# RWKV-7 attention with a gated feed-forward block: chunk 0's diagonal blocks re-laid by PE products, second inverse products on four tile places, a new written order

## The chip, the cores and the metric

The kernel runs on one core of one Trainium2 chip. The metric is the device time of one execution in microseconds (us), lower is better. Inputs and outputs are in DRAM; the core's engines are PE (TensorE, matrix products), DVE (VectorE), ACT (ScalarE), POOL (GpSimd) and SP (SyncE, which here only issues DMAs). Each engine works through its own instructions in the order in which they were written. A product on PE consists of loading a stationary operand (PEld) and streaming a moving one; results go to PSUM, from where DVE or ACT copy them to SBUF.

## The reference

```python
def _attn_ref(r, k, v, w, a, b):            # (4, 8, 768, 40) each
    state = np.zeros((B, H, D, D))
    for t in range(S):
        y[:, :, t] = np.einsum('bhd,bhde->bhe', rt, state)
        Sa = np.einsum('bhde,bhe->bhd', state, at)
        state_decay = state * wt[:, :, None, :] - np.einsum('bhd,bhe->bhde', Sa, bt)
        state = state_decay + np.einsum('bhd,bhe->bhde', vt, kt)
    return y

def _moe_ref(x, w_in, w_out):               # (3072, 320), (320, 2048), (2048, 320)
    h = x @ w_in
    g = h * (1.0 / (1.0 + np.exp(-h)))
    return g @ w_out
```

The attention output is re-ordered to (batch x time, head x channel) and goes through the feed-forward block. 32 pairs of batch and head each carry a state of 40 x 40 through 768 steps. w_in and w_out reach the kernel as 64-bit floats, which it turns into 32-bit ones on the chip.

## The kernel before, in words

**Chunks.** Time is cut into 12 chunks of 64 steps, and each chunk's recurrence is solved in closed form. `load` and `prepare` of a chunk bring its inputs, scan the decay (`down`, `between_`, `up`), scale a, b and k by it, and multiply them with each other (`between`): b with a gives, per pair of batch and head, a strictly triangular 64 x 64 matrix, kept in the tile sb. The chunk needs the inverse of one plus that matrix (tile X). `chain` then solves with X and updates the state G, `read` makes the chunk's output, `bring` re-lays it over DRAM as xt, and `moe` runs the feed-forward block on the 256 rows of the chunk: `full` and `rest` multiply with w_in (lines 1241 and 1254), `gate` applies the activation, `second` multiplies with w_out (line 1281). For chunk 0 the output goes to xt piece by piece from SBUF, without DRAM.

**The inverse.** It is made in one of two ways. Chunks 0 to 2 use `special`: the 16 x 16 blocks on the diagonal are re-laid so that each of 128 partitions holds one whole block. This re-laying is a trip through DRAM: eight DMAs write the blocks from sb to ms (line 543; for chunk 0 four of them go out on ACT's queue, all others on SP's), and one reads them as xs (line 711). DVE inverts the blocks with products and reductions (`dots`, lines 639 and 640) into the tile few, which is ZQ. The way back is a second trip: one DMA writes few to zs (line 719), eight read it into mi, a block-diagonal tile that POOL cleared at the start (line 725). From mi and the rest of sb three rounds of products with additions (`both`, `turn`, `more`; lines 749, 762, 794, 809) make X. For chunk 0 these rounds are cut in two halves. Chunks 3 to 11 are done in pairs by `inverse`: 32 x 32 blocks through DRAM (md, then mi), `dots` on DVE, and back through DRAM (zd, xd) into ZQ and X. `merge` then fills in the block below the diagonal with two groups of 32 products of 32 x 32 (two instructions each): `first` (line 875) and `second` (line 904), each followed by one copy on ACT and one on DVE (lines 257 and 261).

**Tile places.** A product of 32 x 32 uses one of 16 places of the PE array, given by its rows (where its inputs lie) and its columns (where its result goes). The products of `first` are on four places. The products of `second` take rows 32 or 96 and columns 0 or 64, two places in all.

**Weights.** `weights` fetches ten pieces of w_in and w_out as 64-bit words by POOL's DMA queue and turns them into 32-bit floats with steps on DVE and ACT (lines 334 to 370). For the first three pieces the final sum is made by PE with the identity matrix (line 358).

**What sets the order.** Every step is registered with `add` (engine, a cost for the planner, what it reads and writes). The steps get numbers in the order of these calls. The text ORDER lists all numbers in the order in which the instructions are written, and SLOTS gives each use of PSUM or of a rotating buffer its place. Both were searched beforehand by a planner and stand in the kernel as text; the kernel only follows them. So an engine's queue is ORDER restricted to that engine.

**The end.** A count of range checks is multiplied by ones on PE (line 1360) and DVE makes a flag of it (line 1355), which all engines read to skip a fallback path.

Of the kernel before, what the change touches and what calls it, by code (L numbers as in the profile page):

```python
# [10 lines left out]
F32 = mybir.dt.float32  # L11
# [120 lines left out]
"""  # L132

SLOTS = """
21031321312301233211210001321322331332101012301233132222321031202030032332001101131100100023213111111003001230
21301202301012100203001102130131313111033222231221000003311222122330211211120201021320313002303121311000011330
331223200231101300010200110112232231311130303203023110333221023113020311321110200021003021302
"""


@with_exitstack
def kernel(
    ctx: ExitStack,
    tc: tile.TileContext,
    aT: bass.AP,
    kT: bass.AP,
    bT: bass.AP,
    wT: bass.AP,
# [9 lines left out]
    nc = tc.nc  # L158
# [49 lines left out]
    mi = sb.tile([128, 32, 32], F32, name="mi")  # L208
    both_ = sb.tile([128, 2, 32, 32], F32, name="XI")
    XI, tmp = both_[:, 0], both_[:, 1]  # L210
    xs = sb.tile([128, 256], F32, name="xs")
    wc = ring("wc", 3, Q)
    ot = ring("ot", 1, DM)
    pairs = [ps.tile([128, 2, 512], F32, name=f"pair{i}") for i in range(4)]
# [1295 lines left out]
```

## Time and profile before

| | |
|---|---|
| runs of the kernel | 704.92, 702.89, 704.71 us |
| median | 704.71 us |
| the profiled execution | 703.18 us, of which its span is 701.4 us |
| mean granted PE clock in it | 0.997 |
| instructions in it | 27224 |
| moved by DMA | 77.14 MB in 117920 packets |

The profile page has the busy time of each engine, the span in 40 slices, the DMA queues, the chain of work that ended last, and the costliest groups of instructions by line. A row of a group reads: line, engine, operation, output and input tile, shapes, count, then busy time in us and mean duration in ns, then the idle time of the engine just before these instructions and what ended it. A row of the timeline gives the start and the length in us, then the same names; in brackets stands the idle time ahead. Matmul durations include the way through the array, so the distance from one start to the next is the measure of PE's pace. [...]

### The profile page before, as it was taken

To read this page: it belongs to the slowest core of one execution; us is meant where nothing else is said; L and a number is where in the kernel's file an instruction comes from. 1 tells how busy PE (TensorE), PEld (TensorE's weight loads), DVE (VectorE), ACT (ScalarE), POOL (GpSimd) and SP (SyncE) were. 2 spreads that over 40 slices of the span, in tenths; PEclk is the share of its full clock that TensorE was granted. 3 is DMA by queue.
4 is the path that set the end of the run, shared out by engine and by line. 5 is a ranking of instruction groups with operands and counts; after the bars stand their busy time and mean duration, and the time that the engine had idled before them with its cause. 6 is when DMAs were issued, how large, how long until landed. Compare 5 with 4: busy or idle time off the path is not lost.

```text
span 701.4 us, 27224 instructions
## 1 busy us (share of the span) xinstructions
PE 651.2 (93%) x12666; PEld 528.3 (75%) x12666; DVE 415.4 (59%) x612; ACT 194.8 (28%) x243; POOL 13.5 (2%) x31
## 2 busy tenths in 40 slices
PE   0449899999999999999998999999999999999996
PEld 0336688788778778878877778878788778787774
DVE  2887999993896366972447961538953971211000
ACT  4337146244013313114212214203313114021020
POOL 4000010000000000000000000000000000000000
PEclk9999999999999999999999999999999999999998
DMA  9665274763245364163542441642443222211101
GB/s 305 211 161 113 67 219 153 224 145 89 79 141 108 92 150 141 52 165 81 155 101 82 137 107 20 175 127 79 117 124 76 70 72 69 63 42 35 27 1 23
DMA packets 117920, 77.14 MB, mean 110 GB/s; under 512 B 65538, under 2 KB 114229, under 8 KB 117160
## 3 DMA queue, kind: packets, MB, share of 16 engines
q1 hardware_dynamic: 112900, 64.10, 34.7%
q0 software_dynamic: 2224, 10.63, 4.4%
q8 instruction: 101, 1.65, 1.0%
q10 hardware_dynamic: 2676, 0.59, 0.5%
q14 instruction: 19, 0.16, 0.1%
HBM read 60.29 MB, written 14.61 MB: 107 GB/s over the span
## 4 chain that ended last, share of the span: by engine, by line
PE 72%; DVE 10%; DMA 9%; SPq 4%; issue 2%; ACT 2%; ACTq 0%; POOL 0%; DVEq 0%; POOLq 0%
PE pair L1281 23%; PE pair L1241 22%; PE pair L1254 6%; PE pair L1159 3%; PE pair L1105 3%; PE pair L526 2%; DVE XI L639 2%; PE pair L1059 2%; DVE XI L640 2%; PE pair L1144 1%; DMA wz<-in_wT 1%; DMA gts<-in_w_in 1%; PE pair L1002 1%; PE pair L613 1%; PE pair L588 1%
## 5 line engine op out<-in xcount | busy, mean ns | idle before, releaser
L1281 PE MATMUL pair<-wo,gts 128*128 128x320 f32 x768 | 215.3, 436 | 0.2 <-issue 0.2
L1281 PEld LDWEIGHTS pair<-wo,gts 128*128 128x128 f32 x768 | 143.8, 190 | 57.6 <-issue 0.3
L1241 PE MATMUL pair<-xt,wi 128*128 128x256 f32 x768 | 175.4, 383 | 1.8 <-DVE ot L261 1.8
L1241 PEld LDWEIGHTS pair<-xt,wi 128*128 128x128 f32 x768 | 143.7, 190 | 23.8 <-DVE ot L261 1.9
L1264 ACT ACTIVATE gts<-pair 128x1024 f32<-128x1024 f32 x48 | 47.6, 1025 | 69.4 <-PE pair L1254 62.2
L640 DVE TENSOR_REDUCE XI<-XI 128x64 f32<-128x512 f32 (+9 forms) x85 | 58.6, 690 | 2.9
L1117 DVE TENSOR_TENSOR lam<-pair,ml 128x1024 f32<-128x1024 f32 x22 | 26.4, 1220 | 39.9 <-PE pair L1105 39.9
L1254 PE MATMUL pair<-xt,wi 64*128 64x256 f32 x384 | 48.5, 389 | 0.0
L261 DVE COPY ot<-pair 128x320 f32<-128x320 f32 x22 | 10.8, 489 | 62.8 <-PE pair L1281 55.8
L639 DVE TENSOR_TENSOR XI<-XI,mi 128x1024 f32<-128x1024 f32 (+8 forms) x60 | 33.5, 559 | 18.4 <-DMA mi<-md 16.6
L1254 PEld LDWEIGHTS pair<-xt,wi 64*128 64x128 f32 x384 | 35.4, 187 | 5.5 <-issue 0.7
L613 PEld LDWEIGHTS pair<-ident,kb 40*128 40x128 f32 x384 | 16.0, 148 | 20.6 <-DVE kb L508 11.1
L626 ACT COPY kt<-pair 128x640 f32<-128x640 f32 x24 | 16.6, 690 | 51.7 <-PE pair L613 48.9
L613 PE MATMUL pair<-ident,kb 40*128 40x40 f32 x384 | 17.2, 237 | 14.2 <-DVE kb L508 14.2
L508 DVE TENSOR_TENSOR kb<-kbv 128x512 f32<-128x512 f32 (+1 forms) x36 | 29.9, 861 | 0.3
L526 PE MATMUL pair<-a,kb 40*64 40x64 f32 x1536 | 28.4, 228 | 1.5 <-ACT kt L626 0.8
L526 PEld LDWEIGHTS pair<-a,kb 40*64 40x64 f32 x1536 | 25.8, 142 | 4.7 <-issue 1.9
L471 DVE TENSOR_TENSOR_SCAN kbv<-wz,zt 128x1024 f32<-128x1024 f32 x12 | 27.5, 2292 | 0.7
L1105 PEld LDWEIGHTS pair<-r,vut 40*64 40x64 f32 x1536 | 24.2, 135 | 4.5 <-issue 2.5
L489 DVE TENSOR_TENSOR_SCAN wz<-wz,zt 128x1024 f32<-128x1024 f32 x12 | 27.4, 2287 | 0.2
L358 PE MATMUL pair<-gts,ident 128*128 128x512 f32 x16 | 10.6, 767 | 18.0 <-ACT gts L338 18.0
L1105 PE MATMUL pair<-r,vut 40*64 40x64 f32 x1536 | 26.6, 220 | 0.4 <-issue 0.3
(149 smaller groups left out, 672.4 us busy)
## 6 DMA issues: line engine op xcount, KB each, us to landing
wz<-in_wT SPq DMA_DIRECT2D x12, 512.0 KB
kbv<-in_bT SPq DMA_DIRECT2D x12, 512.0 KB
kbv<-in_kT SPq DMA_DIRECT2D x12, 512.0 KB
a<-in_aT SPq DMA_DIRECT2D x12, 512.0 KB
r<-in_rT SPq DMA_DIRECT2D x48, 96.0 KB
vut<-in_vT SPq DMA_DIRECT2D x48, 96.0 KB
vu<-in_v SPq DMA_DIRECT2D x24, 160.0 KB
xh<-lam SPq DMA_DIRECT2D x22, 160.0 KB
```

Source lines behind the costliest of these rows:

```text
L471: nc.vector.tensor_tensor_scan(back(V), back(W[:, 2 : 2 + Q * C]), zt, 1.0, ALU.mult, ALU.add)
L489: nc.vector.tensor_tensor_scan(Z, Z, zt, 0.0, ALU.mult, ALU.add)
L508: TTn[engine].tensor_tensor(out=at_(kb, place(is_b, first), (576 * step, 4 // step), (128, 4), (1, C)), in0=blocks((kf, bf)[is_b]), in1=bl ...
L526: nc.tensor.matmul(room.tile[half(b), j, g * C : g * C + C], lhsT=kb[rows(j), place(is_b, q) : place(is_b, q) + C], rhs=A[rows(j), q * C : ...
L613: nc.tensor.matmul(pt.tile[:, j, g * D : g * D + D], lhsT=kb[rows(j), place(b, q) : place(b, q) + 2 * C], rhs=ident[rows(j), rows(j)], sta ...
L639: nc.vector.tensor_tensor(out=at_(tmp, 0, *dims), in0=x, in1=y, op=ALU.mult)
L640: nc.vector.tensor_reduce(out=out_, in_=at_(tmp, 0, *dims), axis=AX.X, op=ALU.add)
L1105: nc.tensor.matmul(pl.tile[half(1 - b if role else b), b, c * C : c * C + C], lhsT=vut[rows(b), role, hu, :], rhs=rs[rows(b), hh, :], star ...
L1241: nc.tensor.matmul(rooms[g].tile[:, f // 2, (f % 2) * T : (f % 2) * T + T], lhsT=wi[:, k, (4 * g + f) * 128 : (4 * g + f) * 128 + 128], rh ...
L1254: nc.tensor.matmul(rooms[g].tile[:, h, (f % 2) * T : (f % 2) * T + T], lhsT=wi3[half(h), g * 256 + (f % 2) * 128 : g * 256 + (f % 2) * 128 ...
L1264: nc.scalar.activation(out=gts[:, 4 * g * T : 4 * g * T + 4 * T], in_=rooms[g].tile.rearrange("p a b -> p (a b)"), func=AF.Silu)
L1281: nc.tensor.matmul(po[b].tile[:, 0, 0:DM], lhsT=g4[:, f, 128 * b : 128 * b + 128], rhs=wo[:, f, :], start=f == 0, stop=f == NF - 1,)
```

## The change

Four things are changed.

1. **Chunk 0's two trips through DRAM go.** The set TRIP holds the chunks that are treated the new way; it is (0,). `spread` multiplies columns of sb with columns of the identity matrix, in 64 products (128 instructions) on four places, so that each block lands on its partition in PSUM, in two interleaved sets of columns; ACT copies one set, scaled by a mask column of dm, to xs, and DVE adds the other, scaled by a second mask column. The way back: ACT copies the 256 results of few a second time next to themselves (`twice`), `gather` multiplies them with the identity, again 64 products, and one DVE product of 1024 elements with a mask writes mi in full. `masks` fills dm once on DVE. POOL's clearing of mi goes.
2. **The second inverse products** (`second` in `merge`) put their results at columns 64x + 32b instead of 64x, with the order of the loops changed so that neighbours use different places. The copies behind them become two copies of 256 elements each (`united`), on ACT and on DVE.
3. **ORDER and SLOTS are new** throughout. At the start of the new ORDER DVE's steps are: `masks`, then chunk 0's `down`, the scaling of b, `between_`, `up`, the scaling of a, and then the first weight step. In the old one the first weight piece's three steps of bit work and two of another piece stand ahead of chunk 0's `down`. The flag's product stands last on PE in the old ORDER, and before the last `rest` of chunk 9 in the new one.
4. **A variant that is not used** (ADDS is empty): additions in `more` by PE. `more` also names X among what it reads, which it did already in its first round.

```diff
-113 0 138 1 125 3 2 81 77 114 115 116 117 139 118 126 140 158 150 119 141 120 6 127 7 8 9 142 82 11 84 12 28
...
+102 24 0 147 1 114 2 3 70 72 6 9 7 71 8 10 103 14 104 105 15 106 25 148 107 11 115 26 127 108 139 27 73 20 41
...
-        nc.gpsimd.memset(mi, 0.0)
+        if 0 not in TRIP:
+            nc.gpsimd.memset(mi, 0.0)
...
+    TRIP, ADDS = (0,), ()
...
-        if n < NS:
+        if n in TRIP:
+            pass
+        elif n < NS:
...
+        if n in TRIP:
+            pt_ = Room("pair", 3)
+
+            def spread():
+                for t in range(16):
+                    for b in range(2):
+                        for c in range(2):
+                            nc.tensor.matmul(
+                                pt_.tile[64 * b + 32 * c : 64 * b + 32 * c + 32, 0, 32 * t : 32 * t + 32],
+                                lhsT=at_(sbs[i2][half(b)], 16 * c + t, (32, 32)),
+                                rhs=at_(ident[half(b)], 64 * b + 16 * c, (32, 2), (1, 16)),
...
+                                tile_position=(64 * b, 64 * b + 32 * c),
+                            )
...
+            def masks():
+                nc.vector.memset(dm, 1.0)
+                nc.vector.tensor_copy(out=dm[:, 0:3], in_=ml[:, 16:C:16])
+                nc.vector.tensor_tensor(out=dm[:, 1:4], in0=dm[:, 1:4], in1=ml[:, 16:C:16], op=ALU.subtract)
+                for r in range(2):
+                    nc.vector.tensor_reduce(out=dm[:, 4 + r : 5 + r], in_=ident[:, r:128:2], axis=AX.X, op=ALU.add)
...
+                lambda: nc.scalar.activation(out=at_(xs, 0, (16, 16), (1, 16)), in_=own(0), func=AF.Copy, scale=dm[:, 4:5]),
...
+                lambda: nc.vector.scalar_tensor_tensor(
+                    out=at_(xs, 0, (16, 16), (1, 16)), in0=own(1), scalar=dm[:, 5:6], in1=at_(xs, 0, (16, 16), (1, 16)), op0=ALU.mult, op1=ALU.add
+                ),
...
+        if n in TRIP:
+            pz = Room("pair", 2)
+
+            def twice():
+                nc.scalar.copy(out=few[:, 256:512], in_=few[:, 0:256])
+
+            def gather():
+                for t in range(16):
+                    for b in range(2):
+                        for r in range(2):
+                            nc.tensor.matmul(
+                                pz.tile[64 * b + 32 * r : 64 * b + 32 * r + 32, t // 8, t % 8 * C : t % 8 * C + C],
+                                lhsT=at_(few[half(b)], t, (16, 32)),
+                                rhs=ident[half(b), half(b)],
...
+                                tile_position=(64 * b, 64 * b + 32 * r),
+                            )
...
+                lambda: nc.vector.tensor_tensor(
+                    out=at_(DT, 0, (C, Q), (32, 2), (16, 2), (1, 16)),
+                    in0=at_(by_two(pz.tile), 0, (2, Q), (1, 2), (32, 2), (C, 16)),
+                    in1=at_(dm, 0, (0, Q), (2, 2), (1, 2), (0, 16)),
+                    op=ALU.mult,
+                ),
...
         def second():
-            for o in problems("b", "j", "m", "z", "x"):
+            for o in problems("j", "m", "z", "b", "x"):
...
-                    p2.tile[64 * x : 64 * x + 32, x, g * 32 : g * 32 + 32],
+                    p2.tile[64 * x + 32 * b : 64 * x + 32 * b + 32, x, g * 32 : g * 32 + 32],
...
-                    tile_position=(64 * x + 32, 64 * x),
+                    tile_position=(64 * x + 32, 64 * x + 32 * b),
...
+            def united(x=x, R_=R_):
+                for b in range(2):
+                    copy(
+                        ("ACT", "DVE")[x],
+                        X[R_, 8 * b : 8 * b + 8, 32:64],
+                        p2.tile[64 * x + 32 * b : 64 * x + 32 * b + 32, x, 256 * b : 256 * b + 256].rearrange("p (q t) -> p q t", q=8),
+                    )
```

More of the change, by code (lines that the diff above doesn't have):

```diff
@@ L74 @@
 ORDER = """
[57 rows of a table removed]
[56 rows of a table added]
 """
 SLOTS = """
-21031321312301233211210001321322331332101012301233132222321031202030032332001101131100100023213111111003001230
-21301202301012100203001102130131313111033222231221000003311222122330211211120201021320313002303121311000011330
-331223200231101300010200110112232231311130303203023110333221023113020311321110200021003021302
+03032311103303021222110101323023002212120312023311123033303013013000101212230032033133021000301100212123310230
+30212023120223123321310030031003013022110212013210201130302003211310312210110113020131012121113023100120202123
+13231301213030101300002211320113111230333021000112323212232010320300130133012202010110203012033
 """
@@ L211 @@
     xs = sb.tile([128, 256], F32, name="xs")
+    dm = sb.tile([128, 6], F32, name="dm")
     wc = ring("wc", 3, Q)
@@ L709, in special, with own @@
         xsk = ["xs"]
-        dma(
-            lambda: nc.sync.dma_start(xs, ms.rearrange("q s t -> q (s t)")),
-            128,
-            [("ms", b, c) for b in range(2) for c in range(4)],
-            ["xs"],
-            pri,
-        )
+        if n in TRIP:
[8 more added lines that the diff above has]
+                                rhs=at_(ident[half(b)], 64 * b + 16 * c, (32, 2), (1, 16)),
+                                start=True,
+                                stop=True,
+                                tile_position=(64 * b, 64 * b + 32 * c),
+                            )
+            def own(r):
+                return at_(pt_.tile[:, 0], 16 * r, (1, 16), (32, 16))
+            def masks():
[4 more added lines that the diff above has]
+                    nc.vector.tensor_reduce(out=dm[:, 4 + r : 5 + r], in_=ident[:, r:128:2], axis=AX.X, op=ALU.add)
+            if n == min(TRIP):
+                add("DVE", 0.45, masks, [], ["dm"], pri)
+            add("PE", 0.45, spread, [("sb", i2)], [pt_], pri, [pt_], 64, shape="S")
+            add(
+                "ACT",
+                act(256),
+                lambda: nc.scalar.activation(out=at_(xs, 0, (16, 16), (1, 16)), in_=own(0), func=AF.Copy, scale=dm[:, 4:5]),
+                [pt_, "dm"],
+                ["xs"],
+                pri,
+                [pt_],
+            )
+            add(
+                "DVE",
+                vec(256),
+                lambda: nc.vector.scalar_tensor_tensor(
+                    out=at_(xs, 0, (16, 16), (1, 16)), in0=own(1), scalar=dm[:, 5:6], in1=at_(xs, 0, (16, 16), (1, 16)), op0=ALU.mult, op1=ALU.add
+                ),
+                [pt_, "dm"],
+                ["xs"],
+                pri,
+                [pt_],
+            )
+        else:
+            dma(
+                lambda: nc.sync.dma_start(xs, ms.rearrange("q s t -> q (s t)")),
+                128,
+                [("ms", b, c) for b in range(2) for c in range(4)],
+                ["xs"],
+                pri,
+            )
@@ L717, in special @@
         for size, do in steps(16, xs, few, turned):
             add("DVE", 0.36 + 2 * size * 0.00104, do, xsk, [*zq, *tmpk], pri)
-        dma(lambda: nc.sync.dma_start(zs.rearrange("q s t -> q (s t)"), few[:, 0:256]), 128, zq, ["zs"], pri)
-        for b in range(2):
-            for c in range(4):
-                e = "ACT" if n == 0 and b else "SP"
-                p, r = 32 * c + 16 * b, 64 * b + 16 * c
-                dma(
-                    lambda c=c, e=e, p=p, r=r: (nc.scalar if e == "ACT" else nc.sync).dma_start(
-                        mi[r : r + 16].rearrange("s a b -> s (a b)").rearrange("s (q t) -> s q t", q=Q)[:, :, 16 * c : 16 * c + 16],
-                        zs[p : p + 16].rearrange("q s t -> s q t"),
-                    ),
-                    32,
-                    ["zs"],
-                    [("mi", b, c)],
-                    pri,
-                    e,
-                )
+        if n in TRIP:
[10 more added lines that the diff above has]
+                                rhs=ident[half(b), half(b)],
+                                start=True,
+                                stop=True,
+                                tile_position=(64 * b, 64 * b + 32 * r),
+                            )
+            add("ACT", act(256), twice, [], zq, pri)
+            add("PE", 0.6, gather, zq, [pz], pri, [pz], 64, shape="S")
+            add(
+                "DVE",
+                vec(1024),
+                lambda: nc.vector.tensor_tensor(
[4 more added lines that the diff above has]
+                ),
+                [pz, "dm"],
+                [("mi", b, c) for b in range(2) for c in range(4)],
+                pri,
+                [pz],
+            )
+        else:
+            dma(lambda: nc.sync.dma_start(zs.rearrange("q s t -> q (s t)"), few[:, 0:256]), 128, zq, ["zs"], pri)
+            for b in range(2):
+                for c in range(4):
+                    e = "ACT" if n == 0 and b else "SP"
+                    p, r = 32 * c + 16 * b, 64 * b + 16 * c
+                    dma(
+                        lambda c=c, e=e, p=p, r=r: (nc.scalar if e == "ACT" else nc.sync).dma_start(
+                            mi[r : r + 16].rearrange("s a b -> s (a b)").rearrange("s (q t) -> s q t", q=Q)[:, :, 16 * c : 16 * c + 16],
+                            zs[p : p + 16].rearrange("q s t -> s q t"),
+                        ),
+                        32,
+                        ["zs"],
+                        [("mi", b, c)],
+                        pri,
+                        e,
+                    )
@@ L786, in special, with more @@
             src, dst = Xs[i2] if k == 0 else Y[k - 1], Y[k] if k < 2 else Xs[i2]
-            def more(part, py, src=src):
+            plus = n in ADDS
+            def more(part, py, src=src, plus=plus):
+                if plus:
+                    for h in range(2):
+                        nc.tensor.matmul(
+                            of(by_two(py.tile), part)[:, 2 * h : 2 * h + 2] if len(part) == 1 else py.tile[:, h],
+                            lhsT=ident,
+                            rhs=of(Xs[i2], part)[:, 2 * h : 2 * h + 2] if len(part) == 1 else Xs[i2][:, 512 * h : 512 * h + 512],
+                            start=True,
+                            stop=False,
+                            skip_group_check=True,
+                        )
                 for o in problems("b", "m", "z", "j", "x"):
@@ L797, in more @@
                             rhs=src[half(x), c],
-                            start=True,
+                            start=not plus,
                             stop=True,
+                            skip_group_check=plus,
                         )
@@ L804, in special @@
                 l, py = len(part), py_[part]
-                add("PE", 0.92 * l, partial(more, part, py), [*XI_, *(Y_ if k else X_)], [py], pri, [py], 64 * l)
+                add("PE", (0.92 + 0.9 * plus) * l, partial(more, part, py), [*XI_, *(Y_ if k else X_), *X_], [py], pri, [py], 64 * l + 2 * plus)
+                if plus:
+                    add("ACT", act(512 * l), lambda py=py, dst=dst, part=part: copy("ACT", of(dst, part), of(by_two(py.tile), part)), [py], Y_ if k < 2 else X_, pri, [py])
+                    continue
                 add(
@@ L909, in second @@
                     stop=True,
-                    tile_position=(64 * x + 32, 64 * x),
+                    tile_position=(64 * x + 32, 64 * x + 32 * b),
                 )
-        add("PE", 1.0, second, [("Q", 0), ("Q", 1), ("X", i2, 0, 1), ("X", i2, 1, 1)], [p2, ("XM", i2, 0), ("XM", i2, 1)], pri, [p2], 128, shape="S")
+        add("PE", 0.68, second, [("Q", 0), ("Q", 1), ("X", i2, 0, 1), ("X", i2, 1, 1)], [p2, ("XM", i2, 0), ("XM", i2, 1)], pri, [p2], 128, shape="S")
         for x in range(2):
             R_ = slice(64 * x, 64 * x + 32)
-            add(
-                ("ACT", "DVE")[x],
-                act(512),
-                lambda x=x, R_=R_: copy(
-                    ("ACT", "DVE")[x], X[R_, :, 32:64], p2.tile[R_, x].rearrange("p (q t) -> p q t", q=Q)
-                ),
-                [p2],
-                [("XM", i2, x)],
-                pri,
-                [p2],
-            )
+            def united(x=x, R_=R_):
+                for b in range(2):
+                    copy(
+                        ("ACT", "DVE")[x],
+                        X[R_, 8 * b : 8 * b + 8, 32:64],
+                        p2.tile[64 * x + 32 * b : 64 * x + 32 * b + 32, x, 256 * b : 256 * b + 256].rearrange("p (q t) -> p q t", q=8),
+                    )
+            add(("ACT", "DVE")[x], act(512) + 0.2, united, [p2], [("XM", i2, x)], pri, [p2])
     def chain(n):
```

111 rows, old and new, of the table ORDER are left out of this document.

## The prediction

> **What bounds the kernel now.** I read the page first: shares of the engines, slices, chain.
>
> ```profile
> PE 651.2 (93%) x12666; PEld 528.3 (75%) x12666; DVE 415.4 (59%) x612; ACT 194.8 (28%) x243; POOL 13.5 (2%) x31
> ...
> PE   0449899999999999999998999999999999999996
> ```
>
> ```profile
> PE 72%; DVE 10%; DMA 9%; SPq 4%; issue 2%; ACT 2%; ACTq 0%; POOL 0%; DVEq 0%; POOLq 0%
> ```
>
> PE is busy in nearly every slice but the first three and the last, and the chain lies on it for 72% of the span. Then I cut the span into stages with the windows view (length, then busy time of PE, PEld, DVE, ACT, POOL), at the first product of the feed-forward block of chunk 0 and at the end of the last product; the second row is one stretch of the lead-in.
>
> ```profile
> 0.00:88.04 88.04, 48.16 (x1352) 36.09 (x1352) 66.03 (x122) 36.38 (x45) 9.13 (x23) 1.00 0.61 171
> 12.89:79.84 66.95, 39.96 (x1187) 30.79 (x1188) 56.66 (x99) 28.62 (x37) 0.00 (x0) 1.00 0.59 157
> 88.04:694.46 606.42, 602.85 (x11317) 492.14 (x11314) 349.22 (x490) 158.00 (x197) 4.33 (x8) 1.00 0.38 102
> 694.46:701.40 6.94, 0.19 (x3) 0.08 (x2) 0.15 (x1) 0.42 (x1) 0.00 (x0) 0.71 0.16 35
> ```
>
> From 88.04 on PE is idle for 3.6 us in 606: this stage is the sum of the products written into it. In the lead-in PE is idle for 40 of 88 us and DVE sets the pace, with 56.7 busy of the 67 us from 12.89 to 79.84. So the change can gain in two ways: by an earlier start of the long stage, and by shorter products within it. The timeline shows the lead-in's joints (start, length, engine, line):
>
> ```profile
> 12.89 0.69 DVE L334 TENSOR_SCALAR wi<-gts 128x1024 int32<-128x1024 int32 x1 [10.14 <-DMA gts<-in_w_in]
> 14.80 1.23 DVE L336 SCALAR_TENSOR_TENSOR wi<-gts,wi 128x1024 int32<-128x1024 int32 x1 [1.21 <-ACT wi L335]
> ...
> 32.78 1.02 ACT L259 ACTIVATE sb<-pair 128x1024 f32<-128x1024 f32 x1 [0.33 <-PE pair L526]
> ...
> 41.86 0.16 DVE L639 TENSOR_TENSOR XI<-ZQ,xs 128x2 f32<-128x2 f32 x1 [0.63 <-DMA xs<-ms]
> ...
> 47.41 0.69 DVE L640 TENSOR_REDUCE ZQ<-XI 128x64 f32<-128x512 f32 x1
> ...
> 55.54 0.66 PE L762 MATMUL pair<-ident,mi 64*128 64x64 f32 x8 [1.21 <-ACT wi L335]
> ...
> 67.14 0.16 DVE L639 TENSOR_TENSOR XI<-ZQ,xs 128x2 f32<-128x2 f32 x1 [2.76 <-DMA xs<-ms]
> ...
> 79.16 0.68 DVE L1170 TENSOR_TENSOR X<-pair,wz 128x512 f32<-128x512 f32 x1
> ...
> 88.04 1.13 PE L1241 MATMUL pair<-xt,wi 128*128 128x256 f32 x4
> ```
>
> DVE does its setup, waits 10.1 us for the first weight transfer, and only then goes on. Chunk 0's first trip through DRAM runs from the end of the ACT copy (33.80) to 41.86: 8.1 us. The inverse of its blocks ends at 48.10; the second trip lasts until 55.54 at most: 7.4 us. But DVE itself waits just 0.63 us for the first trip: other work fills the rest.
>
> **Part 1, the trips of chunk 0.** Eighteen DMA issues go (ten on SP, eight on ACT), and the clearing of the tile mi on POOL. In come 128 small matmul instructions (spread), an ACT and a DVE copy of 256 elements, an ACT copy of 256, 128 instructions (gather) and a DVE product of 1024; once, some eight tiny mask instructions on DVE. Rows for these:
>
> ```profile
> L738 DVE TENSOR_TENSOR sb<-sb,ml 128x1024 f32<-128x1024 f32 x3 | 3.6, 1216 | 0.0
> ```
>
> ```profile
> 44.53 0.26 DVE L639 TENSOR_TENSOR XI<-ZQ,xs 128x98 f32<-128x98 f32 x1
> ```
>
> ```profile
> 593.20 0.75 PE L875 MATMUL pair<-ZQ,sb 32*32 32x32 f32 x64
> 593.88 1.99 PE L1159 MATMUL pair<-lam,kt 128*40 128x64 f32 x64
> ```
>
> ```profile
> 30.70 1.99 PE L526 MATMUL pair<-a,kb 40*64 40x64 f32 x64
> ```
>
> ```profile
> 121.23 1.16 PE L526 MATMUL pair<-a,kb 40*64 40x64 f32 x64
> ```
>
> A product of 1024 takes DVE 1.22 us; between 98 elements (0.26) and 1024, 256 come to 0.42. The masks I put at 0.9 (bounds 0.5 to 1.5). Products of 32 columns on four places, line 875, start every 10.6 ns (593.20 to 593.88 for 64), so spread is 1.4 us at that pace. The same 64 products of line 526 take 1.99 us at 30.70, after idle time, and 1.16 at 121.23; with that factor of 1.7 spread takes 2.4, which I use. Gather has twice the columns: 2 to 5 us, I take 4. So the first trip of 8.1 becomes 2.4+0.4+0.4 = 3.2, the second 0.4+4+1.2 = 5.6. These times shorten a latency; the end follows DVE's queue, so I sum that.
>
> **Part 2, the written order of the lead-in.** Numbering the calls of add in both versions, I read what each number of the order stands for. Up to the second of the two products that finish chunk 0's output (79.16 above) DVE has the same 64 steps, plus four: masks 0.9, the copy 0.4, the product 1.2, and one weight step moved up, 1.2. That is 3.7, so 60.4 busy instead of 56.7. What differs is the start: the scan of chunk 0's decay now stands ahead of all weight steps. Its input is the first transfer on SP:
>
> ```profile
> q1 hardware_dynamic: 889, 0.89, 54.8%
> ```
>
> That is the DMA view cut at 5.0 us: 0.89 MB moved by then, the first 0.51 MB being this input. I let DVE start at 5.5 (bounds 5 to 8); masks stands ahead of it, and where its own input, a constant from POOL, is later, DVE starts later within these bounds. Of the 10.3 us not busy in 12.89 to 79.84 some 2 are gaps between tiny instructions; they stay. Waits that I can place in the new order: 1.1 for ACT's first weight step (as at 14.80), 0.6 for spread with its ACT copy, and 0.8 allowed for the rest. DVE's steps end at 5.5+60.4+2+2.5 = 70.4 instead of 79.84: **9.4 us**. Bounds: all 10.3 idle and the start at 8 give 78.7, a gain of 1.1; start at 5 and 1 us idle give 66.4, a gain of 13.4.
>
> Is a transfer late next? Chunk 1 keeps its trips. Adding up DVE's steps in the new order, its factors are ready at 38 (33 us of steps and waits from 5.5), its ACT copy ends at 41, and xs lands at 53: the first trip's 8.1, and 4 allowed for SP, which alone issues all eight pieces with two loads among them. DVE, added up the same way, reaches chunk 1's blocks at 54. The cover is 1 us; where it fails, DVE stands. Ahead of these pieces SP also holds chunk 2's b, which waits until DVE has used chunk 1's, just before 38; vu and r of chunk 0 are queued behind it, and their first readers on PE come later still.
>
> From 79.84 to 88.04 lie 8.2 us in which the output pieces travel and PE does weight sums and chunk 1's blocks. In the new order two of the sums, 1 us each, stand earlier; I take 7.3 (bounds 5.5 to 8.2). The first feed-forward product starts at 77.7: 10.3 us earlier. All PE products ahead of it are the same in both orders, but for spread and gather.
>
> **Part 3, the second inverse products.** Nine chunks, 64 instructions each, on two places now and on four after:
>
> ```profile
> 612.91 1.20 PE L904 MATMUL pair<-X,ZQ 32*32 32x32 f32 x64
> 614.04 1.14 PE L947 MATMUL pair<-G,a 40*64 40x40 f32 x64
> ```
>
> 1.13 us from start to start here, 0.68 for line 875, which has the same shape on four places: 0.45 less, nine times: **4.05 us**, all on PE in the dense stage. The copies behind them are halved:
>
> ```profile
> L257 ACT COPY ZQ<-pair 32x512 f32<-32x512 f32 x9 | 5.2, 576 | 39.9 <-PE pair L875 39.8
> L261 DVE COPY X<-pair 32x512 f32<-32x512 f32 x9 | 6.2, 689 | 15.6 <-ACT X L257 12.8 <-PE pair L904 2.7
> ```
>
> Two of 256 cost about 0.15 to 0.2 more than one of 512 (estimate from 0.42 each on DVE). Behind them waits the solve of that chunk; in the new order at least one block of other products lies between. Without that cover it would be 9 x 0.2 = 1.8.
>
> [...]
>
> **Part 4, the order from 88 on and the end.** PE's products are the same; the order leaves more PE work between chunk outputs and the feed-forward products that fetch them. Of the 3.6 us idle I count 0 back (bounds -3.6 to +6, the latter half a us at each of twelve chunks).
>
> ```profile
> 694.46 0.19 PE L1360 MATMUL pair<-ones,count 128*1 128x1 f32 x2
> 694.56 0.42 ACT L257 COPY ot<-pair 128x320 f32<-128x320 f32 x1 [3.88 <-PE pair L1281]
> 694.76 0.15 DVE L1355 TENSOR_SCALAR bad<-pair 1x1 int32<-1x1 f32 x1 [31.48 <-PE pair L1360]
> ```
>
> The flag's product stood last on PE; now it comes earlier, so the engines can read the flag at once instead of at 694.9. The last store starts as before. I take 0.3 (0 to 0.5).
>
> **Sum:** 10.3+4.05+0.3 = 14.7 off the profiled execution, 703.18 (span 701.4 and 1.8 around it): 688.5. The runs shown have a median of 704.71, 1.5 above it; I stay at 688.5.
>
> **Rivals.** *The lead-in gain is given back.* DVE's idle time returns behind chunk 1's trip (cover 1 us) or behind PE at its slow pace (1.99 for 1.16). For it: 10.3 idle now, queues in order. Against: only 3.4 of that was waiting for xs. With half to nearly all returned the lead-in gains 1 to 6: 693 to 698. Chance 0.19.
>
> *The second products gain nothing*, were their starts bound per instruction: 692.6. The pace of line 875 speaks against it. Chance 0.08.
>
> *The search found more:* the waits of 88 on go (3.6) and DVE's idle too (lead-in 13.4): 682. Chance 0.05.
>
> *Slower: the inverse becomes the bound.* The chain shows that the solve of chunk 3 already follows a load directly:
>
> ```profile
> 222.31 4.37 DMA X<-xd
> 226.73 1.13 PE pair L1002 x62
> ```
>
> Between chunk 4's first product and this solve the new order has two PE steps fewer (2.0 us with the shorter second products) and one DVE product more (1.2). With the load's 4.37 exposed as well, PE would stand 7.6 us, at five inverses 38 us: 727. It decides from 14.7/5 = 3 us each. Against it: of SP's other transfers nine stand between the last two of these six loads today, none in the new order. Chance 0.05.
>
> **How the numbers follow.** Forecast 684 to 693: 0.60; rivals as given; 0.03 for no change, all gains returned. A measurement of this kernel tells about 0.3%, 2 us, from none. Faster 0.92, same 0.03, slower 0.05. The range goes from 683 (dense waits gone) to 697.5 (lead-in gain at its lower bound of 1.1).
>
> **What would show it.** DVE's first scan near 5.5 instead of 20.54; chunk 0's dots starting near 21; the first product of line 1241's successor near 78; 64 second products in 0.68; PE idle of 3 to 4 us from there. It is wrong if DVE stands for xs of chunk 1 by more than 2 us, or if PE stands before chunk 3's solve.

## The result, and the profile after

The changed kernel takes 723.57 us (median of 723.56, 723.58, 727.82 and 720.34); the kernel before, run beside it, 704.0 us. The ratio is 1.028, 95% interval 1.023 to 1.034: **slower by 2.8%**, where 2.2% faster was forecast. The profiled execution took 723.56 us, its span 721.8.

From the page of the changed kernel, the busy shares, the granted clock by slices and the chain:

```profile
PE 667.0 (92%) x12922; PEld 539.2 (75%) x12922; DVE 419.7 (58%) x628; ACT 198.3 (27%) x254; POOL 12.5 (2%) x30
...
PEclk9969999999999899999999999999999999999999
...
PE 90%; issue 4%; DVE 4%; DMA 1%; ACT 0%; DVEq 0%; ACTq 0%
```

The chain now lies on PE for 90% of the span, and 4% are "issue", time in which PE waited for nothing that the profile shows. The clock, 1.00 before up to the last product, has dips. Cut at the same joints as before (windows view: length, then busy time of PE, PEld, DVE, ACT, POOL, then clock, DMA share, GB/s):

```profile
0.00:82.69 82.69, 57.09 (x1609) 44.74 (x1609) 68.12 (x124) 37.66 (x47) 9.54 (x25) 0.92 0.61 176
82.69:716.30 633.61, 609.80 (x11318) 494.45 (x11314) 351.59 (x504) 160.23 (x206) 2.96 (x6) 0.99 0.37 98
716.30:721.80 5.50, 0.08 (x1) 0.00 (x0) 0.00 (x0) 0.43 (x1) 0.00 (x0) 0.85 0.13 31
```

The lead-in gained 5.35 us (88.04 to 82.69), half of the forecast 10.3. The long stage, with the same number of PE products, grew from 606.42 to 633.61: **27.2 us more where 4.05 less was forecast**. PE is idle in it for 23.8 us instead of 3.6. What it waited for, over the whole span of the changed kernel (waits view: engine and line, what it waited for, us in total, times, longest), and then, for comparison, in the long stage of the kernel before:

```profile
PE pair L1076 <- issue: 4.7, 3, 1.9
PE pair L528 <- issue: 3.4, 3, 2.4
...
PE pair L1010 <- issue: 2.8, 2, 1.5
PE pair L981 <- issue: 2.7, 3, 1.0
PE pair L1264 <- issue: 2.4, 3, 1.5
```

```profile
PE pair L1241 <- DVE ot L261: 1.8, 1, 1.8
PE pair L526 <- DVE ot L261: 0.6, 1, 0.6
PE pair L947 <- issue: 0.4, 1, 0.4
PE pair L1059 <- issue: 0.3, 1, 0.3
```

In this stage no engine and no load is waited for. Its idle stretches of PE of over 0.25 us, listed from the single records of the trace (**gaps** from here on), are 21, together 23.5 us, all "issue"; before, the issue gaps of that size come to 0.7 us. They hit products of every kind, and in the middle of a step. The PE timeline of two of them:

```profile
242.70 1.51 PE L528 MATMUL pair<-a,kb 40*64 40x64 f32 x86
246.65 1.44 PE L528 MATMUL pair<-a,kb 40*64 40x64 f32 x42 [2.44 <-issue]
...
263.20 0.60 PE L1010 MATMUL pair<-X,ZQ 32*32 32x32 f32 x46
265.33 0.37 PE L1010 MATMUL pair<-X,ZQ 32*32 32x32 f32 x18 [1.53 <-issue]
265.63 4.54 PE L1346 MATMUL pair<-xt,wi 128*128 128x256 f32 x12
```

A run of 128 equal MATMUL instructions (two steps of 64) breaks off after 86, in the middle of its second step, and goes on 2.4 us later; operands and room were there from that step's start. So I counted instructions. Two windows of the changed kernel that end just ahead of these two stalls, and the page's row of the queue that carries PE's instructions:

```profile
0.00:246.60 246.60, 213.03 (x4934) 173.32 (x4935) 191.92 (x298) 93.87 (x116) 12.49 (x30) 0.97 0.54 153
0.00:265.30 265.30, 230.18 (x5190) 185.81 (x5190) 201.58 (x312) 96.95 (x120) 12.49 (x30) 0.96 0.53 147
```

```profile
q8 instruction: 103, 1.69, 1.0%
```

Loads and products together are 9869 at the first and 10380 at the second, 511 apart; with the one semaphore instruction between them, which these columns leave out, 512. Counted in this way with the semaphore instructions, **all 21 stalls stand at one remainder, 193, of the instruction number divided by 256**. And 1.69 MB in 103 packets is 16.4 KB each, one packet for each 256 instructions. In the trace's single DMA packets the n-th packet belongs to the n-th such boundary: PE goes on 1.2 to 1.5 us after its packet has ended, in all 21 cases; where the packet ended over 1.7 us ahead of the boundary, no gap exceeds 0.3. For the stall at 246.65 it ran from 244.22 to 245.12.

So the theory to test (**theory 1**): PE gets its instructions in blocks of 256. In the changed kernel the packet of a block starts, in the median, 1.0 us after PE has entered the block before it, takes 1.1, and PE goes on 1.2 at least after its end: some 3.3 us in all. Behind 85 us the blocks of the changed kernel last from 2.7 to 29.0 us: the long ones hold wide feed-forward products, and there the packet has time. A block that is nearly all small products is through sooner, and then PE stands at the boundary. Where boundaries fall is set by the number of instructions written ahead, so the same order can be good or bad. Against it stood the **rivals** that the new order crowds small products wherever it is cut (rival 2), and that the halved clock of the lead-in was the cause (rival 4; it shows as clock 0.54 from 37 to 52 us).

### The profile page after: what moved, and what is told of

Its sections match the earlier page's. It is cut to its first block, busy times and chain, and to the rows that moved or that the text cites. A ratio compares the mean times of both kernels' runs of the same rounds, so it can differ in the third digit from the quotient of the medians.

```text
span 721.8 us, 27739 instructions
## 1 busy us (share of the span) xinstructions
PE 667.0 (92%) x12922; PEld 539.2 (75%) x12922; DVE 419.7 (58%) x628; ACT 198.3 (27%) x254; POOL 12.5 (2%) x30
## 3 DMA queue, kind: packets, MB, share of 16 engines
q8 instruction: 103, 1.69, 1.0%
## 4 chain that ended last, share of the span: by engine, by line
PE 90%; issue 4%; DVE 4%; DMA 1%; ACT 0%; DVEq 0%; ACTq 0%
PE pair L1386 30%; PE pair L1346 24%; PE pair L1359 6%; PE pair L528 4%; PE pair L1210 3%; PE pair L1264 3%; PE pair L896 3%; PE pair L1164 2%; PE pair L617 2%; PE pair L592 2%; PE pair L1107 2%; PE pair L1076 2%; PE pair L1052 2%; PE pair L1249 2%; PE pair L360 1%
## 5 line engine op out<-in xcount | busy, mean ns | idle before, releaser
L1346 PE MATMUL pair<-xt,wi 128*128 128x256 f32 x768 | 178.5, 388 | 0.0
L1346 PEld LDWEIGHTS pair<-xt,wi 128*128 128x128 f32 x768 | 146.1, 193 | 23.6 <-issue 0.7
L528 PE MATMUL pair<-a,kb 40*64 40x64 f32 x1536 | 32.0, 235 | 20.3 <-DVE a L500 13.7
L528 PEld LDWEIGHTS pair<-a,kb 40*64 40x64 f32 x1536 | 28.2, 147 | 24.3 <-issue 19.3
L1275 DVE TENSOR_TENSOR lam<-pair,wz 128x1024 f32<-128x1024 f32 x11 | 13.5, 1223 | 27.4 <-PE pair L1264 27.4
L259 ACT ACTIVATE sb<-pair 128x1024 f32<-128x1024 f32 x12 | 12.3, 1025 | 53.3 <-PE pair L528 53.3
L643 DVE TENSOR_TENSOR XI<-XI,xs 128x1024 f32<-128x1024 f32 (+1 forms) x25 | 25.2, 1010 | 0.7
```

The costliest lines, as they stand in the source:

```text
L528: nc.tensor.matmul(room.tile[half(b), j, g * C : g * C + C], lhsT=kb[rows(j), place(is_b, q) : place(is_b, q) + C], rhs=A[rows(j), q * C : ...
L643: nc.vector.tensor_tensor(out=at_(tmp, 0, *dims), in0=x, in1=y, op=ALU.mult)
L1346: nc.tensor.matmul(rooms[g].tile[:, f // 2, (f % 2) * T : (f % 2) * T + T], lhsT=wi[:, k, (4 * g + f) * 128 : (4 * g + f) * 128 + 128], rh ...
```

## The experiments

Each but the last adds instructions at one place: products that are done more than once, with the same values. In the experiments lines stand one later (L1347 for L1346), in the two with wide products ten or eleven.

```diff
-        def between(is_b, room):
-            for o in problems("m", "z", "x", "b", "j"):
+        def between(is_b, room, again=0):
+            todo = list(problems("m", "z", "x", "b", "j"))
+            for o in todo[: again % 32] + todo * (1 + again // 32):
...
-        add("PE", 0.9, partial(between, 0, pk), ["K", ("a", i3)], [pk], pri + 0.5, [pk, sk], 128)
+        add("PE", 0.9, partial(between, 0, pk, 32 if n == 0 else 0), ["K", ("a", i3)], [pk], pri + 0.5, [pk, sk], 128)
```

One product is four instructions (two loads, two MATMUL), so 32 are 128 instructions, half a block. The step is chunk 0's product of K and A, at 33 us in both kernels, with 3 to 4.6 us of idle PE behind it.

**128 more (half a block), in the changed kernel.**

> The changed kernel, with all 32 products of chunk 0's K times A done twice (same values; 128 more TensorE instructions in the lead-in, in an idle stretch of 3 us, so that everything behind them stands 128 instructions later in the stream). Theory 1, TensorE waits at fixed boundaries of 256 instructions and the new order stands half a block off: counted from the trace of the changed kernel, with 3.6 us as the least time of a block, the stalls behind 82.7 us fall from 24 us to 11, the gaps called issue from 23.7 us to about 5 to 12, and the half-clock stretches with them; time 700 to 712. Rival 2, the new order as such crowds small products wherever it stands: 723 to 725. Rival 4, only the halved clock of the lead-in: at most 4 us less, 719 to 724.

Measured: **687.93 us** against 702.04 for the kernel before, ratio 0.980 (0.973 to 0.986). Waits on "issue" that are left in its whole span, and its stages (the 3.2 us of L618 come at 24 us, ahead of the added products, and are in the changed kernel too):

```profile
PE pair L618 <- issue: 3.2, 1, 3.2
PE pair L529 <- issue: 3.2, 2, 2.5
...
PE pair L1211 <- issue: 0.8, 1, 0.8
```

```profile
0.00:78.16 78.16, 56.39 (x1673) 44.37 (x1673) 67.93 (x124) 37.63 (x47) 9.61 (x25) 0.93 0.63 186
78.16:681.30 603.14, 599.84 (x11317) 489.00 (x11314) 351.49 (x504) 159.86 (x206) 2.90 (x6) 1.00 0.38 103
681.30:686.70 5.40, 0.04 (x1) 0.00 (x0) 0.00 (x0) 0.42 (x1) 0.00 (x0) 0.77 0.13 32
```

More work, about 36 us less time, and less than the span that I had given. Behind the first feed-forward product two gaps are left, 3.2 us together, at 103.7 and 113.9, again at remainder 193. Rivals 2 and 4 forbade this. The same 64 instructions of the second inverse products that were torn apart at 265 stand whole here:

```profile
251.31 0.75 PE L1011 MATMUL pair<-X,ZQ 32*32 32x32 f32 x64
252.00 7.17 PE L1347 MATMUL pair<-xt,wi 128*128 128x256 f32 x32
```

**256 more (a whole block): the control.** The edit with 64 instead of 32.

> The control: the same edit with the products done three times (256 more instructions, a whole block, and 2.2 us more TensorE work in the idle 3 us). Theory 1: the boundaries fall between the same instructions as in the changed kernel behind the lead-in, the stalls there stay at 22 to 25 us, time 718 to 725. Rival 2: also 718 to 725. Rival 4: if covering the idle 3 us with products is what helps, this one helps more than 128 instructions do. If both this and the 128 come down alike, theory 1 falls.

Measured: 720.75 us, 20 gaps behind the first feed-forward product, 19.7 us; ratio 1.028 (1.021 to 1.035). Twice as many added products, and hardly any of the gain: it is the position that counts. Some boundaries again fall inside the same steps, such as L1011 at 256 and 473 us.

**128 more in the kernel before.**

> The kernel before, with the same 128 instructions added at the same place. Theory 1: the order of before is thrown half a block off; counted from the trace of before in the same way, its stalls rise from 8 to 27 us: 715 to 728. Rivals 2 and 4: 703 to 706, since TensorE stands idle for 4.6 us behind that place.

Measured: **731.73 us**, ratio 1.040 (1.034 to 1.046); a little above the expected span. The kernel before has become as bad as the changed one, with waits that it never had:

```profile
PE pair L1003 <- issue: 5.3, 2, 2.7
PE pair L1106 <- issue: 3.6, 3, 1.3
PE pair L972 <- issue: 3.5, 2, 2.5
PE pair L527 <- issue: 3.4, 2, 1.8
```

**256 more in the kernel before.**

> The control on the kernel before: its chunk 0 products done three times, 256 more instructions, a whole block. Theory 1: the boundaries fall as they did, gaps behind the lead-in 3 to 6 us, 702 to 707. If the slowdown of 128 instructions came from more TensorE work in the lead-in, this one is slower still: over 730.

Measured: 703.34 against 703.38 us, ratio 1.001 (0.999 to 1.003), with no issue gap of 0.25 us in the long stage. Adding work in the lead-in costs the kernel before nothing; shifting it by half a block costs 4%.

**128 more, but in the middle of the changed kernel.** The condition is n == 6 instead of n == 0.

> The changed kernel with the same 128 instructions added not in the lead-in but in chunk 6's K times A, which the changed kernel issues near 297 us. Theory 1 (position in the instruction stream): the stalls ahead of that place stay as they were (about 10 us of gaps between 83 and 297 us), those behind it are gone (at most 3 us of the 13.5); time 706 to 713. Rival 2 (the new order as such; the gain of the first run came from the lead-in and what followed from it): 721 to 726.

Measured: 707.05 us (ten executions, from 699.59 to 712.36; the traced one took 710.77), ratio 1.002 (0.999 to 1.005). What it waited for on "issue" from 86 to 300 us (first fence, the largest rows), and from 304 to the end:

```profile
PE pair L529 <- issue: 2.8, 2, 2.4
PE pair L1265 <- issue: 2.0, 3, 0.9
PE pair L1108 <- issue: 1.7, 2, 1.1
```

```profile
PE pair L1077 <- issue: 0.3, 1, 0.3
```

Ahead of the added instructions the gaps come to 10.3 us to 297 (10.2 in the changed kernel), with two more around them, at 298.5 and 302.5, of 1.7 together; behind, 0.3 instead of 13.3. One kernel, one order: bad up to the place where the count shifts, good from there on.

**64, 192 and 160 more, at the first place.**

> The changed kernel with half of those products done twice (64 more instructions). Theory 1, by the same count: the stalls rise from 24 to 30 us, time 724 to 732, so that 64 instructions make it slower and 128 faster. Rivals 2 and 4: 720 to 724.

> The changed kernel with 192 more instructions at the place of the first run (48 of chunk 0's K times A products more). Counted again from the trace of the changed kernel with its stalls taken out, now with 3.2 us as the least time from one boundary to the next (the least stretch that ends in a stall is 2.9 us there): behind 82.7 us 15.5 us of stalls with nothing added (23.5 measured), 18.9 with 64 (15.0 measured), 5.9 with 128 (3.2 measured), 11.4 with 192, 15.5 again with 256 (19.7 measured). So theory 1: gaps of 8 to 16 us, time 694 to 708. Rival: what counted was only to be off the old boundary by far, and 192 is as good as 128: under 5 us, 687 to 691.

> The same with 160 more instructions: by the same count 6.2 us of stalls, as good as 128. Theory 1: gaps of 2 to 8 us, time 686 to 695.

| added to the changed kernel | gaps behind the first feed-forward product, us | the execution with these gaps, us | median time, us | before beside it, us |
|---|---|---|---|---|
| 0 | 23.5 | 723.56 | 723.57 | 704.0 |
| 64 | 15.0 | 708.56 | 713.82 | 702.04 |
| 128 | 3.2 | 688.61 | 687.93 | 702.04 |
| 160 | 7.3 | 698.04 | 696.06 | 703.75 |
| 192 | 17.8 | 716.74 | 718.29 | 703.75 |
| 256 | 19.7 | 714.92 | 720.75 | 702.04 |

The gaps are those of one execution; from one to the next the time of one kernel varies by some 10 us where there are many of them (714.92 to 725.34 with 256 added). The versions with 160 and 192 ran twice each.

All three missed their time: 64 was expected to make it slower and made it 10 us faster, 192 came out 10 us above its span, 160 one. My count took one least time for all blocks, but the packet's start varies. Behind 85 us it lies up to 5.3 us after PE's entry into the block before, and can also lie ahead of that entry, by up to 5.7 us: in the kernel before 24 of 89 packets start ahead of it and with 128 added to the changed one 31 of 88, but in the changed one 5 of 89 and in the kernel before with 128 added 9 of 90. So a good position is one at which the next block is often asked for early; what starts a packet early, no run shows. The count shows that half a block is best; for the amounts in between it is too coarse.

**Wide products in the idle stretch: is it the lead-in's clock?** The 32 added products, each 160 columns wide, ahead of the true ones.

```diff
+            for o in problems("m", "z", "x", "b", "j") if wide else ():
...
+                nc.tensor.matmul(
+                    room.tile[half(b), j, 0:wide],
+                    lhsT=kb[rows(j), place(is_b, q) : place(is_b, q) + C],
+                    rhs=A[rows(j), 0:wide],
```

> The changed kernel with 32 added products as in the first run, but each 160 columns wide, on top of the true ones: again 128 instructions, so the order stands on the right boundaries, and some 3 us more TensorE work in the idle stretch from 34.5 to 37.5 us. If the halved clock there is what the lead-in still loses, the clock reads 1.00 from 37 to 52 us, chunk 0's first inverse products take 2.1 us instead of 3.7, the first feed-forward product comes at 74 to 76 us instead of 78.2, and the time is 683 to 686. If the lead-in is bound by VectorE or a transfer all the same, the first feed-forward product stays at 77 to 78.5 and the time at 686 to 689.

Measured: 688.77 us, ratio 0.980 (0.977 to 0.983), so the version with half a block added stands a second time at 2% under the kernel before. But the clock from 37 to 52 us was 0.77, not 1.00, and the first feed-forward product came at 79.02, later than either case expected. The next run has the same lead-in, and there the clock did recover:

**The second inverse products back on two places.** The wide products stay; `second` and the copies behind it are those of the kernel before.

```diff
-            for o in problems("j", "m", "z", "b", "x"):
+            for o in problems("b", "j", "m", "z", "x"):
...
-                    p2.tile[64 * x + 32 * b : 64 * x + 32 * b + 32, x, g * 32 : g * 32 + 32],
+                    p2.tile[64 * x : 64 * x + 32, x, g * 32 : g * 32 + 32],
...
-                    tile_position=(64 * x + 32, 64 * x + 32 * b),
+                    tile_position=(64 * x + 32, 64 * x),
```

> The run with the wide products, with one part of the change undone: the second inverse products on two places of TensorE again with one copy per half (9 times 64 products; the count of instructions is the same). By the step of the prediction: each stretch of 64 takes 1.13 us instead of 0.68, together 4.05 us, and the time is 3 to 5 us longer than with the wide products alone. Rival: the products are hidden or the second copies cost what they save: within 1 us.

Measured: 693.28 us, 4.5 more than with the wide products alone (six executions each, from 690.79 to 696.98 here and from 687.75 to 694.32 there). The group of the second products, first with four places (wide products alone), then with two:

```profile
L1020 PE MATMUL pair<-X,ZQ 32*32 32x32 f32 x576 | 6.8, 194 | 0.0
```

```profile
L1020 PE MATMUL pair<-X,ZQ 32*32 32x32 f32 x576 | 10.8, 192 | 0.0
```

4.0 us on PE: the term of the prediction, and the medians agree with it. And in the traced execution the clock of the lead-in recovered early. Its window from 37 to 52 us, its PE timeline, and a row of its DVE timeline:

```profile
37.00:52.00 15.00, 13.99 (x480) 13.09 (x480) 14.51 (x18) 9.85 (x13) 0.00 (x0) 0.89 0.44 109
```

```profile
44.10 2.32 PE L906 MATMUL pair<-X,XI 64*64 64x64 f32 x64
...
63.12 0.34 PE L1221 MATMUL pair<-r,vut 40*64 40x64 f32 x6 [0.73 <-issue]
...
68.13 0.83 PE L602 MATMUL pair<-vu,lam 64*64 64x40 f32 x41 [0.71 <-issue]
...
78.80 3.72 PE L1357 MATMUL pair<-xt,wi 128*128 128x256 f32 x16
```

```profile
53.57 0.16 DVE L653 TENSOR_TENSOR XI<-ZQ,xs 128x2 f32<-128x2 f32 x1 [0.73 <-DMA xs<-ms]
```

The first inverse products take 2.32 us instead of 3.68 and start 1.2 earlier than in the first run, yet the first feed-forward product comes at 78.80, not before 78.16. PE stood at four block boundaries between 52 and 69 us, 2.6 us in all (two of them in the rows above), and DVE stood 0.73 us for chunk 1's blocks, a wait that the first run does not have: one microsecond earlier, and the transfer is late. So in this execution an earlier clock brought no earlier end; what it would bring without those boundaries, no run shows. For the long stage, where the loss is, rival 4 has nothing left: half a block and a whole one, added in the same place, part by 33 us.

## Why the prediction was wrong

**The step that failed is part 4:** "PE's products are the same; ... Of the 3.6 us idle I count 0 back (bounds -3.6 to +6 ...)". The products are the same, but I took PE's time as their sum plus waits for data, with no term for the supply of instructions: that wait was put at nothing, and it measured 23.5 us. The 27.2 us by which the long stage grew add up as follows. Idle time: 23.8 instead of 3.6, 20.2 more. The clock: three stalls were followed by halved clock, in rows of the changed kernel,

```profile
240.00:260.00 20.00, 17.56 (x205) 12.58 (x206) 10.89 (x17) 2.75 (x4) 0.00 (x0) 0.83 0.55 146
260.00:280.00 20.00, 18.20 (x433) 15.34 (x431) 5.05 (x11) 6.77 (x11) 0.00 (x0) 0.91 0.46 119
540.00:560.00 20.00, 18.20 (x406) 15.49 (x400) 3.06 (x5) 7.73 (x11) 0.00 (x0) 0.91 0.29 64
```

and one minus the clock, times 20 us, is 3.4, 1.8 and 1.8, together 7.0; this is an upper value, since PE was idle for a part of these stretches. Less 4.05 for the second products: 23.2. The remaining 4 I put down to the products ahead of the 21 stalls, whose own 0.2 us (mean 194 to 235 ns) is otherwise covered by the next; this is an estimate. The version with half a block added has the same order: its long stage is 30.5 us shorter, of which PE's idle time is 20.5 and its busy time 10.0.

The bounds of +6 were made from "half a us at each of twelve chunks", for waits on data. The true cost lay outside them since it has another cause. The forecast's own lower end, 683, does not follow from its reason either: 688.5 less the 3.6 us of dense waits is 684.9. Nothing hangs on it here.

**The lead-in, part 2: its sum held, its first feed-forward product did not.** DVE's first scan starts at 5.51 (5.5), chunk 0's first dots at 21.22 (near 21), the two PE steps spread and gather take 2.05 and 2.17 (2.4 and 4 taken). Then "All PE products ahead of it are the same in both orders" failed in the same way. PE rows of the changed kernel:

```profile
43.86 0.69 PE L528 MATMUL pair<-a,kb 40*64 40x64 f32 x11 [0.56 <-issue]
...
59.17 0.90 PE L1076 MATMUL pair<-R,X 64*64 64x40 f32 x44 [1.90 <-issue]
...
68.87 0.35 PE L1164 MATMUL pair<-vu,kt 128*40 128x40 f32 x6 [0.89 <-issue]
...
77.42 0.69 PE L839 MATMUL pair<-mi,sb 64*64 64x64 f32 x29 [0.56 <-issue]
...
82.69 3.72 PE L1346 MATMUL pair<-xt,wi 128*128 128x256 f32 x16
```

These are 3.9 us of the 5.0 by which 82.69 misses 77.7. DVE's waits for PE from 46 to 75 us come to 6.9 us here and to 2.6 with half a block added, so PE's stalls were passed on to DVE, with the slower clock (0.54 from 37 to 52 us, 0.66 with half a block added) as a possible further part. With half a block added the two steps that finish chunk 0's output end at 70.85 (70.4 forecast) and the first feed-forward product comes 7.3 us later (7.3), at 78.16. The transfer of chunk 1's blocks, whose cover I put at 1 us, is waited for in neither; with half a block added PE waits 0.4 us for the way back (L840, mi<-zs).

**Part 3 was right:** 0.69 us for 64 (251.31 to 252.00), 4.0 in all; with four places a start follows every 10.8 ns.

**The end** gained 1.4 (6.94 to 5.50), not 0.3; where the other 1.1 come from was not followed.

**The rivals.** None was it. The first one's number for the lead-in (1 to 6 us gained) fits the 5.35, and DVE did stand behind a slow PE; but it left the long stage as it was. The slower one, at 727, is near the measured time by chance: its wait, PE for the load X<-xd ahead of the solves, is in no row of the waits. What was missing is a rival of the kind that the trace of before already hinted at: its few "issue" waits in the long stage, 0.4 and 0.3 us, which the prediction does not mention.

**On the aligned order the forecast stands:** 78.16 + 603.14 + 5.40 is a span of 686.7, and 688.5 less the 1.8 around the span is 686.7. The terms: 77.7, 606.42 - 4.05 = 602.4 and 6.6. They miss by 0.5, 0.7 and -1.2, so that the sum fits to a tenth is chance; in the long stage 3.2 us of stalls took the place of waits on DVE that went. That each term is within 1.2 us is not: what the change does was read rightly, and what it costs to put it into a stream of instructions was left out.

Why this order stands half a block off is argued, not shown: for PE steps `add` is given a count behind the rooms, 128 for the 32 products of `between`, which is their number of instructions, but `spread` and `gather` give 64 each and issue 256. That is 384 too few, a block and a half. An order searched with an eye on the boundaries and with these counts would be off by just the 128 that put it right; how it was searched is not in the kernel.

## What to carry to other kernels

Where the bounding engine runs through hundreds of small instructions, its instruction supply can cost time, as it did here with 23.5 us of 723.6: count instructions per microsecond, and look at which boundaries idle time labelled "issue" falls. An order tuned to a fraction of a per cent may be tuned to its position in the stream too: 128 instructions ahead of it, useless ones in idle time, cost one order here 4% and gained the other nearly 5%. The test is cheap: add a half block and a whole one, and if the two differ, it is the position.

## What the runs showed of the hardware

- PE's instructions came in packets of 16.4 KB, one for each 256 of them, and little ahead: in none of the twelve traces behind 85 us does a packet start before PE has entered the second block ahead of its own; in the traces of the two kernels the earliest starts 3.0 us after that (before) and 3.8 (changed). In the kernel before, the crossings cost 0.7 us in all in the long stage, in the changed one 23.5 us of 723.6.
- The packet started later where data traffic was high. Over all twelve traces, for the 880 blocks behind 85 us whose packet started no more than 0.6 us ahead of PE's entry into the block before, take the busy share of the DMA engines within 1 us of that entry: with the share under 0.1 (391 blocks) the median start is 0.78 us after it, with 0.9 and more (87 blocks) 1.55 us. The longest stall of the changed kernel's long stage, the one that ends at 246.65, had its packet 4.27 us after it (239.95), while input loads ran (DMA share 1.03 from 239.95 to 244.22). That traffic delays it is a reading of this relation; no run changed the traffic.
- Halved clock followed some single stalls of over a microsecond and not others; their length alone did not decide it. The stretch from 552.9 to 556.3 us of the changed kernel runs at 0.50, behind a gap of 1.75; gaps of 1.53 and 2.44 also brought one (0.50 from 266.2 to 269.6 and from 245.7 to 252.5), 1.51 and 1.49 did not. In other runs a gap of 1.15 us brought one (at 256 us, 256 added) and one of 2.61 did not (at 426 us, 64 added).
